# K and V blocks of 2 MB from one buffer arena, and wq and wo 2 MB at once, in a four-pass attention kernel

## The chip, the cores and the metric

The kernel runs on one core of one Trainium2 chip. The metric is the device time of the whole program in microseconds; lower is better. Engines are named as the profile names them: PE is TensorE (matmul), PEld its weight loads, DVE is VectorE, ACT is ScalarE, POOL is GpSimd, SP is SyncE, which issues the loads here. The build gives each engine a queue of instructions of its own; "DMA" means the 16 DMA engines of the core.

## The reference

Forward and backward of attention, MLP, attention, MLP for one token, with the same weights and the same K and V caches in both layers. What matters is the traffic: K and V are 4 heads x 65536 rows x 128 columns in bfloat16, 64 MiB each, and have to be read several times, because a softmax over all rows lies between them.

```python
x = x + A(layernorm(x), k_cache, v_cache, wq, wo)   # 32 query heads on 4 K/V heads, 65536 keys
x = x + B(layernorm(x), w1, b1, w2, b2)             # relu squared, 1024 -> 3584 -> 1024
x = x + A(layernorm(x), k_cache, v_cache, wq, wo)
x = x + B(layernorm(x), w1, b1, w2, b2)
# outputs: x and the gradients of all inputs (those of K and V are 64 MiB each)
```

The kernel goes over K and V four times: pass 1 and pass 2 are the forward attentions, pass 3 the backward of the second layer, pass 4 the rest with the stores of both cache gradients. Between the passes lie three dense phases with the MLP weights.

## The kernel before

K, V, weights and outgoing blocks share 12 buffer parts of 1 MiB (8 KB in each of 128 partitions). A load is traced where its block is first used; SP runs ahead of the compute engines as far as parts and semaphores allow.

```python
    BLK = J * DH                                   # J = 32 rows of 128: 8 KB in a partition
    SLOTS = [(slotp, "slot%d" % i) for i in range(NSLOT)]     # NSLOT = 12
    ...
    def kv8(t, g, c8):                             # 8 chunks of a K or V block, loaded at its first use
        b, j = divmod(c8, J)
        key = (t, g, b)
        if key not in KV["have"]:
            sl = Slot("blk_" + t)
            v = sl.t[:, :].rearrange("p (j d) -> p j d", d=DH)
            nc.sync.dma_start(out=v, in_=KVIN[t][g][b])
            KV["have"][key] = (sl, v)
        return KV["have"][key][1][:, j:j + 8, :]
```

A forward pass is a software pipeline over groups of 8 chunks. `kT` transposes K on PE and copies the result out of PSUM on ACT or DVE (`evac` balances a load count); `kS` makes the scores from a copy two steps old. After every 16 groups `stats` finds the maximum and ACT computes 8 exponentials of 128x128. `v8` multiplies V by them 23 steps after the K of the same rows.

```python
        def kT(g, c8):
            kb8 = kv8("k", g, c8)
            pt = ps_tr()
            for i in range(8):
                nc.tensor.transpose(pt[:, i, :], kb8[:, i, :], ident_b[:, :])
            kv_done("k", g, c8)                    # gives the part back after its last use
            kt = ktpool.tile([P, 8, P], BF, name="kt", tag="kt")      # 4 buffers
            evac(kt[:, :, :], pt[:, :, :])         # ACT or DVE
            state[(g, c8)] = kt
        ...
        def stats(g, su):
            ...                                    # DVE, PE, DVE, PE, DVE: the maximum over partitions
            for h in range(R):                     # R = 8
                nc.scalar.activation(out=E(g, c0, SU)[:, :, L["lr"].start + h], in_=S[:, h, :], func=ACTF.Exp,
                                     bias=negm[:, g, su, h:h + 1], scale=SCALE, accum_out=rs[:, h:h + 1])
        ...
        pipeline(items, [(kT, 0), (kS, TLEAD), (v8, FWD_LAG)], bg, end)     # lags 0, 2, 23
```

Of the kernel before, what the change touches and what calls it, by code (L numbers as in the profile page):

```python
# [10 lines left out]
BF = mybir.dt.bfloat16  # L11
# [5 lines left out]
P = 128  # L17
# [3 lines left out]
def kernel(  # L21
# [24 lines left out]
    nc = tc.nc  # L46
    D = A_x.shape[-1]
    G = A_k_cache.shape[1]
    SK = A_k_cache.shape[2]
    DH = A_k_cache.shape[3]  # L50
    QD = A_wq.shape[1]
    HQ = QD // DH
    R = HQ // G
    F = B_w1.shape[1]
    DC, FC = D // P, F // P
    C = SK // P
    J = 32
    NB = C // J
    SU = min(128, C)
# [7 lines left out]
    STORE_STEPS = 5  # L67
    WAIT_STEPS = 5
    NSLOT = 12
# [6 lines left out]
    epool = ctx.enter_context(tc.tile_pool(name="epool", bufs=1))  # L76
    ktpool = ctx.enter_context(tc.tile_pool(name="ktpool", bufs=4))
    mvs = ctx.enter_context(tc.tile_pool(name="mvs", bufs=2))
    slotp = ctx.enter_context(tc.tile_pool(name="slotp", bufs=1))
# [14 lines left out]
    def ps_gg():  # L94
        return PS["pool"].tile([P, 512], F32, name="ps_gg", tag="gg", bufs=4)

    def ps_acc(shape):
        return PS["pool"].tile(shape, F32, name="ps_acc", tag="acc", bufs=1)
# [30 lines left out]
    load = {"act": 0.0, "dve": 0.0, "pe": 0.0}  # L129
# [108 lines left out]


    BLK = J * DH  # L240
    SLOTS = [(slotp, "slot%d" % i) for i in range(NSLOT)]
    FREE = [(0, i) for i in range(NSLOT)]
    NOW = {"step": 0}

    class Slot:
        def __init__(self, name, fill=False):
            n = 0
            if fill:
                ready = [k for k, (at, _) in enumerate(FREE) if at <= NOW["step"] - 1]
                n = ready[-1] if ready else 0  # L250
            self.i = FREE.pop(n)[1]
            pool, tag = SLOTS[self.i]
            self.t = pool.tile([P, BLK], BF, name=name, tag=tag)

        def free(self, stored=False):

            give_slot(self.i, STORE_STEPS if stored else 0)

    def give_slot(i, more=0):
        NOW["step"] += 0.01  # L260
        insort(FREE, (NOW["step"] + more, i))

    def add_slot(pool, tag):
        SLOTS.append((pool, tag))
        give_slot(len(SLOTS) - 1)

    def kv_views(ap):
        return [ap[0, g].rearrange("(b p j) d -> b p j d", p=P, j=J) for g in range(G)]

    KVIN = {"k": kv_views(A_k_cache), "v": kv_views(A_v_cache)}  # L270
    GKv = kv_views(out_2)
    GVv = kv_views(out_3)

    KV = {"have": {}, "keep": set()}

    def kv8(t, g, c8):
        b, j = divmod(c8, J)
        key = (t, g, b)
        if key not in KV["have"]:
            sl = Slot("blk_" + t)  # L280
            v = sl.t[:, :].rearrange("p (j d) -> p j d", d=DH)
            nc.sync.dma_start(out=v, in_=KVIN[t][g][b])
            KV["have"][key] = (sl, v)
        return KV["have"][key][1][:, j:j + 8, :]

    def kv_done(t, g, c8):

        key = (t, g, c8 // J)
        if c8 % J == J - 8 and key not in KV["keep"]:
            KV["have"].pop(key)[0].free()  # L290

    def order_by_unit(desc, unit):
        out = []
# [7 lines left out]
    def touch_order(items, stages):  # L301
        seen, out = set(), []
        maxlag = max(l for _, l in stages)
        for i in range(len(items) + maxlag):
            for t, lag in stages:
# [13 lines left out]
    TOUCH = [touch_order(ITEMS[0], [("k", 0), ("v", FWD_LAG)]), touch_order(ITEMS[1], [("k", 0), ("v", FWD_LAG)]),  # L319
             touch_order(ITEMS[2], [("v", 0), ("k", B3_LAG)]), touch_order(ITEMS[3], [("v", 0), ("k", B4_LAG)])]  # L320

    def plan_keep(p):
        if p == 3:
            return set()
        last = TOUCH[p][-(NKEEP + 2):]
        return set([k for k in TOUCH[p + 1] if k in last][:NKEEP])
# [9 lines left out]
    def rows_of(W):  # L336
        return W.rearrange("(kc p) n -> p kc n", p=P)
# [1 line left out]
    def f_rows_of(W):  # L339
        return W.rearrange("(s p j) n -> p s j n", p=P, j=4)  # L340

    def slabs(name, load, nk, kper, ncols, ahead=1):
        pend = deque()
        ks = deque(range(0, nk, kper))

        def fetch():
            k = ks.popleft()
            kn = min(kper, nk - k)
            sl = Slot(name)
            v = sl.t[:, 0:kn * ncols].rearrange("p (k n) -> p k n", n=ncols)  # L350
            nc.sync.dma_start(out=v, in_=load(k, kn))
            pend.append((k, kn, sl, v))

        def gen():
            while ks or pend:
                while ks and len(pend) < ahead:
                    fetch()
                k, kn, sl, v = pend.popleft()
                for kk in range(kn):
                    yield k + kk, v[:, kk, :]  # L360
                sl.free()
        g = gen()
        g_fetch = [fetch for _ in range(ahead)]
        return g, g_fetch
# [7 lines left out]

    def wq_slabs(g, ahead=1):
        v = rows_of(A_wq)
        return slabs("s_wq", lambda k, kn: v[:, k:k + kn, g * 1024:(g + 1) * 1024], DC, 4, 1024, ahead)

    def wo_slabs(g, ahead=1):
        v = rows_of(A_wo)
        return slabs("s_wo", lambda k, kn: v[:, g * R + k:g * R + k + kn, :], R, 4, 1024, ahead)

    def w1_slabs(ahead=1):
        v = rows_of(B_w1)
# [276 lines left out]
    def pipeline(items, stages, bg, end=()):  # L659
        maxlag = max(l for _, l in stages)  # L660
        for i in range(len(items) + maxlag):
            for fn, lag in stages:
                if 0 <= i - lag < len(items):
                    fn(*items[i - lag])
            bg.step(i)
            NOW["step"] += 1
            for before, fn in end:
                if i == len(items) + maxlag - before:
                    fn()
# [16 lines left out]
    EH = max(SU, C // 2)  # L686
    ETILE = {}
# [8 lines left out]
    def E_done(g, c0, n):  # L696

        if c0 % EH == 0 and EH * R2 == BLK:
            add_slot(epool, "E%d_%d" % (g, c0 // EH))

    def gsl(g):
        return slice(g * R, (g + 1) * R)
# [50 lines left out]
    def attn_fwd(p, L, on_group, bg, end=()):  # L753
# [3 lines left out]
        state = {}  # L757
# [121 lines left out]
                    nc.scalar.activation(out=L["fw"][:, g, :, :], in_=fd[:], func=ACTF.Exp)  # L879

        KV["keep"] = plan_keep(p)
        pipeline(items, [(kT, 0), (kS, TLEAD), (v8, FWD_LAG)], bg, end)
        st.close()

# [17 lines left out]
    def attn_bwd3(p, L, on_group, bg, end=()):  # L902
# [5 lines left out]
        state = {}  # L908
# [56 lines left out]
                    on_group(g)  # L965

        KV["keep"] = plan_keep(p)
        pipeline(items, [(vT, 0), (vS, TLEAD), (k8, B3_LAG)], bg, end)
        st.close()


    def attn_bwd4(p, La, Lb, on_group, bg, stack, end=()):
# [8 lines left out]
        state = {}  # L981
# [84 lines left out]
        def outer16(name, out, key, xt, gg, j1):  # L1066

            if j1 == 0:
                state[key] = Slot(name, True)
            stg = state[key].t[:, :].rearrange("p (j d) -> p j d", d=DH)  # L1070
            for m in range(2):
                pgs = [ps_gg(), ps_gg()]
                for h in range(2):
                    nc.tensor.matmul(pgs[h][:, :], lhsT=xt[64 * h:64 * h + 64, j1 // 8 + m, :],  # L1074
                                     rhs=gg[64 * h:64 * h + 64, :, :].rearrange("p a b -> p (a b)"),
                                     start=True, stop=True, tile_position=(64 * h, 0))
                for h in range(2):
                    jj = j1 + 8 * m + 4 * h
                    evac(stg[:, jj:jj + 4, :].rearrange("p j d -> p (j d)"), pgs[h][:, :], kind="f32")
            if j1 + 16 == J:  # L1080
                nc.gpsimd.dma_start(out=out, in_=stg)
                state.pop(key).free(stored=True)

        def dV8(g, c8):
            b, j0 = divmod(c8, J)
            if 2 * j0 < J:
                outer16("gstv", GVv[g][b], "stv", state[("xe", g, b)], state[("GG", g, c8 // SU)][1], 2 * j0)

        def k8(g, c8):
            kb8 = kv8("k", g, c8)  # L1090
            b, j0 = divmod(c8, J)
            su = c8 // SU
            X, xt = state[("xd", g, b)]
            if c8 == sufirst[(g, su)]:
                state["ps_dq"] = ps_acc([P, 4, R2])
            ps_dq = state["ps_dq"]
            for i in range(8):
                c = c8 + i
                s = c % J
                w = min(4, J - s)  # L1100
                nc.tensor.matmul(ps_dq[:, 0:w, :].rearrange("p a b -> p (a b)"), lhsT=kb8[:, i, :],  # L1101
                                 rhs=X[:, s:s + w, :].rearrange("p a b -> p (a b)"),
                                 start=(c == sufirst[(g, su)]), stop=(c == sulast[(g, su)] + 7), skip_group_check=True)
            kv_done("k", g, c8)
            if c8 == sulast[(g, su)]:
                fold_dq(La, g, su, ps_dq[:, 0, 0:R], gfirst[g] // SU == su, glast[g] // SU == su, dspool)
                if glast[g] // SU == su:
                    on_group(g)
            if 2 * j0 >= J:
                outer16("gstk", GKv[g][b], "stk", xt, state[("GG", g, su)][0], 2 * j0 - J)  # L1110

        KV["keep"] = plan_keep(p)
        pipeline(items, [(vT, 0), (vS, TLEAD), (dV8, DV_LAG), (k8, B4_LAG)], bg, end)


# [325 lines left out]
```

## Time and profile before

| | before |
|---|---|
| time, median of 3 runs | 2035.71 us (2035.61 to 2037.0) |
| moved by DMA | 803.5 MB, 395 GB/s over the span |
| DMA share in the passes | 1.01 (passes 1 to 3), 0.97 (pass 4) |
| PE busy | 83% of the span |

From the page of the kernel before: the engines' busy time, and the span in 40 slices (PEclk is the clock granted to TensorE, DMA the share in tenths, GB/s the rate).

```profile
span 2035.9 us, 69009 instructions
...
PE 1689.3 (83%) x30754; PEld 1344.3 (66%) x30754; DVE 1188.6 (58%) x2586; ACT 1103.0 (54%) x2063; POOL 92.4 (5%) x232
...
DMA  9999999999999998999999986999999999999995
GB/s 384 416 410 414 413 414 415 360 335 406 411 414 413 413 415 323 398 415 410 416 412 414 416 338 231 375 424 393 422 424 424 423 423 404 423 415 423 423 371 212
```

The rate is nearly flat within a pass, 410 to 416 GB/s in passes 1 to 3 and mostly 422 to 424 in pass 4, and falls most in the dense phases (the 360 335, 323 and 338 231) and at the end. The windows view gives passes 1, 2 and 3, from the first transpose to the last matmul on a cache block; the last three columns are PE's clock, DMA share and GB/s.

```profile
core 0: us, PE busy (x) PEld busy (x) DVE busy (x) ACT busy (x) POOL busy (x), PEclk, DMA share, GB/s
12.50:378.10 365.60, 296.47 (x6658) 280.70 (x6659) 168.10 (x387) 175.40 (x387) 0.29 (x1) 0.93 1.01 411
433.30:781.20 347.90, 285.60 (x6587) 270.76 (x6585) 165.89 (x382) 173.71 (x385) 0.29 (x1) 0.93 1.01 406
833.30:1197.70 364.40, 296.62 (x6510) 265.76 (x6506) 170.96 (x327) 151.06 (x186) 0.67 (x1) 0.96 1.01 412
```

PE has 60 to 70 us of idle time in each forward pass. The waits view of PE says for what it waited (us in total, times, longest), and SP's own waits say what held the next load back.

```profile
PE ps_sc L792 <- DVE kt L153: 38.8, 26, 2.4
...
PE ps_sc L792 <- ACT kt L150: 11.5, 33, 1.8
...
PE ps_tr L774 <- DMA blk_k<-in_A_k_cache_dram: 3.3, 3, 1.4
```

```profile
SPq L282 <- DMA blk_k<-in_A_k_cache_dram: 215.3, 112, 4.3
SPq L282 <- DMA blk_v<-in_A_v_cache_dram: 206.8, 113, 4.4
...
SPq L282 <- PE ps_tr L774: 117.8, 77, 5.4
```

Of the waits before a load of K or V, those for earlier loads to land are the longest (422 us together; the waits of SP for stores, such as 279.9 us for `gstv`, belong to pass 4), and the DMA share is 1.01: DMA is the limit. In pass 2 alone (433.3 to 781.2 us) SP already waits longer for PE to give parts back, 146 us, than for loads, 84 us:

```profile
SPq L282 <- PE ps_acc L858: 76.2, 31, 8.1
SPq L282 <- PE ps_tr L774: 70.1, 41, 5.1
SPq L282 <- DMA blk_k<-in_A_k_cache_dram: 43.1, 22, 2.1
SPq L282 <- DMA blk_v<-in_A_v_cache_dram: 40.6, 23, 3.1
```

PE hardly ever waits for a K block (3.3 us in two passes).

### The profile page before, as it was taken

How to read it: one execution, taken by the hardware profiler on the slowest of the kernel's cores; microseconds unless marked ns; L12 is line 12 of the kernel's file. 1: busy time of each engine (PE TensorE's matmuls, PEld its weight loads, DVE VectorE, ACT ScalarE, POOL GpSimd, SP SyncE). 2: the span in 40 equal slices, each digit the busy share in tenths (PEclk: the TensorE clock that was granted, in tenths of full speed). 3: DMA queues.
4: the chain of work that ended last, by engine and by line, in shares of the span. 5: the costliest groups of instructions: out<-in, count | busy, mean ns of one | idle time of the engine just before them, and what ended most of it. 6: DMA issues, size and time to landing. Idle time of an engine off the chain costs nothing.

```text
span 2035.9 us, 69009 instructions
## 1 busy us (share of the span) xinstructions
PE 1689.3 (83%) x30754; PEld 1344.3 (66%) x30754; DVE 1188.6 (58%) x2586; ACT 1103.0 (54%) x2063; POOL 92.4 (5%) x232
## 2 busy tenths in 40 slices
PE   7888887688788886887978888979988978898897
PEld 6778777688787776776867777545544545454454
DVE  4444454255444542555464446867967877687775
ACT  3544454255444542445354345767766766576675
POOL 0000000000000000000000000101101111010111
PEclk9999899799899996999999988988988998698898
DMA  9999999999999998999999986999999999999995
GB/s 384 416 410 414 413 414 415 360 335 406 411 414 413 413 415 323 398 415 410 416 412 414 416 338 231 375 424 393 422 424 424 423 423 404 423 415 423 423 371 212
DMA packets 136536, 803.50 MB, mean 395 GB/s; under 512 B 12448, under 2 KB 12462, under 8 KB 52398
## 3 DMA queue, kind: packets, MB, share of 16 engines
q1 hardware_dynamic: 112190, 633.39, 76.9%
q0 software_dynamic: 24048, 165.70, 19.6%
q8 instruction: 240, 3.93, 0.8%
q14 instruction: 58, 0.48, 0.1%
HBM read 633.35 MB, written 165.69 MB: 392 GB/s over the span
## 4 chain that ended last, share of the span: by engine, by line
PE 45%; DMA 28%; ACT 15%; DVE 8%; issue 4%; SPq 0%; ACTq 0%; POOLq 0%; DVEq 0%; POOL 0%
DMA blk_v<-in_A_v_cache_dram 13%; PE ps_tr L774 7%; ACT E L831 6%; DMA blk_k<-in_A_k_cache_dram 5%; PE ps_sc L792 5%; PE ps_tr L1026 4%; PE ps_gg L1074 4%; PE ps_acc L858 4%; ACT kt L150 4%; PE ps_tr L917 3%; DVE kt L153 3%; DMA out_dram<-og 3%; PE ps_gg L1139 2%; DMA out_dram<-gstk 2%; PE ps_mv L397 2%
## 5 line engine op out<-in xcount | busy, mean ns | idle before, releaser
L153 DVE COPY kt<-ps_tr 128x1024 bf16<-128x1024 bf16 x751 | 507.3, 687 | 340.6 <-PE ps_tr L774 145.4
L150 ACT COPY kt<-ps_tr 128x1024 bf16<-128x1024 bf16 x273 | 275.7, 1024 | 410.9 <-PE ps_tr L774 230.0
L774 PE MATMUL ps_tr<-ident_b,blk_k 128*128 128x128 bf16 x4096 | 297.3, 226 | 4.3 <-DMA blk_k<-in_A_k_cache_dram 3.3
L150 ACT CAST gstk<-ps_gg 128x512 bf16<-128x512 f32 x396 | 207.6, 600 | 99.7 <-PE ps_gg L1074 78.5
L150 ACT CAST gstv<-ps_gg 128x512 bf16<-128x512 f32 x379 | 199.2, 601 | 100.1 <-PE ps_gg L1074 99.2
L774 PEld LDWEIGHTS <-blk_k 128*128 128x128 bf16 x4096 | 249.5, 102 | 4.9 <-DMA blk_k<-in_A_k_cache_dram 3.8
L792 PE MATMUL ps_sc<-L_qpad,kt 128*128 128x64 bf16 (+7 forms) x4096 | 197.4, 194 | 52.8 <-DVE kt L153 38.8
L1074 PE MATMUL ps_gg<-GG,xt 64*128 64x512 bf16 x1024 | 211.5, 403 | 21.2 <-ACT gstk L150 11.0
L792 PEld LDWEIGHTS <-kt 128*128 128x128 bf16 x4096 | 158.8, 100 | 71.3 <-DVE kt L153 45.7
L858 PE MATMUL ps_acc<-E,blk_v 128*128 128x64 bf16 (+4 forms) x4096 | 177.6, 200 | 33.0 <-issue 10.9
L1026 PEld LDWEIGHTS <-blk_v 128*128 128x128 bf16 x2048 | 128.5, 103 | 108.0 <-issue 83.0
L1026 PE MATMUL ps_tr<-ident_b,blk_v 128*128 128x128 bf16 x2048 | 183.0, 230 | 20.1 <-DMA blk_v<-in_A_v_cache_dram 18.9
L858 PEld LDWEIGHTS <-blk_v 128*128 128x128 bf16 x4096 | 152.9, 103 | 36.4 <-issue 31.3
L831 ACT ACTIVATE E<-S_sb,L_negm 128x128 bf16<-128x128 f32 x256 | 150.4, 990 | 38.2 <-DVE L_negm L827 38.1
L1101 PEld LDWEIGHTS <-blk_k 128*128 128x128 bf16 x2048 | 84.3, 100 | 115.7 <-issue 87.0
L917 PE MATMUL ps_tr<-ident_b,blk_v 128*128 128x128 bf16 x2048 | 143.7, 224 | 14.3 <-DMA blk_v<-in_A_v_cache_dram 12.0
L917 PEld LDWEIGHTS <-blk_v 128*128 128x128 bf16 x2048 | 121.4, 100 | 31.1 <-DMA blk_v<-in_A_v_cache_dram 20.6
L1101 PE MATMUL ps_acc<-X,blk_k 128*128 128x64 bf16 (+3 forms) x2048 | 119.2, 196 | 23.0 <-DMA blk_k<-in_A_k_cache_dram 23.0
L831 ACT ACTIVATION_READ_ACCUMULATOR E<-S_sb,L_negm 128x1 f32 x256 | 123.5, 483 | 0.0
L937 PE MATMUL ps_sc<-dOpad,kt 128*128 128x64 bf16 (+7 forms) x2048 | 100.7, 194 | 26.6 <-ACT kt L150 15.5
L1055 PE MATMUL ps_sc<-DOB,kt 128*128 128x64 bf16 (+3 forms) x2048 | 111.3, 198 | 0.2 <-DVE kt L153 0.2
L153 DVE CAST gstv<-ps_gg 128x512 bf16<-128x512 f32 x133 | 90.0, 684 | 28.1 <-PE ps_gg L1074 27.7
(271 smaller groups left out, 2203.0 us busy)
## 6 DMA issues: line engine op xcount, KB each, us to landing
blk_k<-in_A_k_cache_dram SPq DMA_DIRECT2D x248, 1024.0 KB, 20.1
blk_v<-in_A_v_cache_dram SPq DMA_DIRECT2D x243, 1024.0 KB, 20.2
out_dram<-gstv POOLq DMA_DIRECT2D x64, 1024.0 KB, 13.1
out_dram<-gstk POOLq DMA_DIRECT2D x64, 1024.0 KB, 12.5
s_wq<-in_A_wq_dram SPq DMA_DIRECT2D x32, 1024.0 KB, 18.8
s_wo<-in_A_wo_dram SPq DMA_DIRECT2D x32, 1024.0 KB, 20.2
s_w<-in_B_w_dram SPq DMA_DIRECT2D x32, 896.0 KB, 7.8
out_dram<-og POOLq DMA_DIRECT2D x23, 1024.0 KB, 13.9
```

The source lines that it names most:

```text
L150: nc.scalar.copy(out=out, in_=in_)
L153: nc.vector.tensor_copy(out=out, in_=in_)
L774: nc.tensor.transpose(pt[:, i, :], kb8[:, i, :], ident_b[:, :])
L792: nc.tensor.matmul(state["ps_s"][:, s:s + w, :].rearrange("p a b -> p (a b)"), lhsT=kt[:, i, :], rhs=L["qpad"][:, g, 0:w, :].rearrange("p ...
L831: nc.scalar.activation(out=E(g, c0, SU)[:, :, L["lr"].start + h], in_=S[:, h, :], func=ACTF.Exp, bias=negm[:, g, su, h:h + 1], scale=SCALE ...
L858: nc.tensor.matmul(ps_o[:, 0:w, :], lhsT=vb8[:, i, :], rhs=E(g, c, w)[:, :, lr], start=(c % SU == 0), stop=(c % SU == SU - 1), skip_group_ ...
L917: nc.tensor.transpose(pt[:, i, :], vb8[:, i, :], ident_b[:, :])
L937: nc.tensor.matmul(state["ps_dp"][:, s:s + w, :].rearrange("p a b -> p (a b)"), lhsT=vt[:, i, :], rhs=dOpad[:, g, 0:w, :].rearrange("p a b ...
L1026: nc.tensor.transpose(pt[:, i, :], vb8[:, i, :], ident_b[:, :])
L1055: nc.tensor.matmul(state["ps_dp"][:, s:s + w, :].rearrange("p a b -> p (a b)"), lhsT=vt[:, i, :], rhs=DOB[:, g, 0:w, :].rearrange("p a b - ...
L1074: nc.tensor.matmul(pgs[h][:, :], lhsT=xt[64 * h:64 * h + 64, j1 // 8 + m, :], rhs=gg[64 * h:64 * h + 64, :, :].rearrange("p a b -> p (a b) ...
L1101: nc.tensor.matmul(ps_dq[:, 0:w, :].rearrange("p a b -> p (a b)"), lhsT=kb8[:, i, :], rhs=X[:, s:s + w, :].rearrange("p a b -> p (a b)"), ...
```

## The change

The intent is fewer, larger DMA packets. A K or V block may now take two neighbouring parts of an arena, with one load of 16 KB per partition. If no pair is free, if the block's other half is there already, or in pass 4, halves are loaded as before. In the passes wq and wo also come 2 MB at once (their packets stay 2 KB). For this the rows of a block are laid out so that a half is an 8 KB run at a 16 KB pitch in DRAM. Dense weights take the part that has been free longest.

```diff
-    SLOTS = [(slotp, "slot%d" % i) for i in range(NSLOT)]
-    FREE = [(0, i) for i in range(NSLOT)]
+    JW = 2 * J
+    ARENA = slotp.tile([P, NSLOT * BLK], BF, name="arena")
+    GRAN = [ARENA[:, i * BLK:(i + 1) * BLK] for i in range(NSLOT)]
+    FREE = {i: 0.0 for i in range(NSLOT)}
+    def take_pair():
+        both = [(max(FREE[i], FREE[i + 1]), i) for i in range(0, NSLOT, 2) if i in FREE and i + 1 in FREE]
+        ...
     def kv_views(ap):
-        return [ap[0, g].rearrange("(b p j) d -> b p j d", p=P, j=J) for g in range(G)]
+        return [ap[0, g].rearrange("(b p j) d -> b p j d", p=P, j=JW) for g in range(G)]
     ...
+            if NOW["pairs"] and hb % 2 == 0 and (t, g, hb + 1) not in have:
+                i = take_pair()
+            if i is None:
+                sl = Slot("blk_" + t)
+                nc.sync.dma_start(out=sl.t.rearrange("p (j d) -> p j d", d=DH), in_=half(KVIN[t], g, hb))
+                have[key] = sl
+            else:
+                for h in range(2):
+                    have[(t, g, hb + h)] = Slot("blk_" + t, at=i + h)
+                if key in KV["halves"]:            # the last blocks of a pass: two 1 MB loads
+                    ...
+                else:
+                    nc.sync.dma_start(out=wide(i).rearrange("p (j d) -> p j d", d=DH), in_=KVIN[t][g][hb // 2])
     ...
 # slabs() for wq and wo: 2 * kper rows in a pair, where NOW["wide"]
     ...
     def pipeline(items, stages, bg, end=()):
         for i in range(len(items) + maxlag):
+            NOW["wide"] = NOW["pairs"]
     ...
+        NOW["pairs"] = p < 3
```

The hunks left out adapt names, the gradients' views and the freeing of pairs.

More of the change, by code (lines that the diff above doesn't have):

```diff
@@ L240 @@
     BLK = J * DH
-    SLOTS = [(slotp, "slot%d" % i) for i in range(NSLOT)]
-    FREE = [(0, i) for i in range(NSLOT)]
-    NOW = {"step": 0}
-    class Slot:
-        def __init__(self, name, fill=False):
-            n = 0
-            if fill:
-                ready = [k for k, (at, _) in enumerate(FREE) if at <= NOW["step"] - 1]
-                n = ready[-1] if ready else 0
-            self.i = FREE.pop(n)[1]
-            pool, tag = SLOTS[self.i]
-            self.t = pool.tile([P, BLK], BF, name=name, tag=tag)
+    JW = 2 * J
@@ new lines, with wide @@
+    ARENA = slotp.tile([P, NSLOT * BLK], BF, name="arena")
+    GRAN = [ARENA[:, i * BLK:(i + 1) * BLK] for i in range(NSLOT)]
+    FREE = {i: 0.0 for i in range(NSLOT)}
+    NOW = {"step": 0, "pairs": True, "wide": False}
+    def wide(i):
+        return ARENA[:, i * BLK:(i + 2) * BLK]
+    def take_pair():
+        both = [(max(FREE[i], FREE[i + 1]), i) for i in range(0, NSLOT, 2) if i in FREE and i + 1 in FREE]
+        if not both:
+            return None
+        i = min(both)[1]
+        del FREE[i], FREE[i + 1]
+        return i
@@ new lines, in take_one, with __init__ @@
+    def take_one(fill):
+        by_age = sorted((t, i) for i, t in FREE.items())
+        if fill:
+            ready = [i for t, i in by_age if t <= NOW["step"] - 1]
+            i = ready[-1] if ready else by_age[0][1]
+        else:
+            i = by_age[0][1]
+        del FREE[i]
+        return i
+    class Slot:
+        def __init__(self, name, fill=False, at=None, both=False):
+            self.i = take_one(fill) if at is None else at
+            self.n = 2 if both else 1
+            self.t = wide(self.i) if both else GRAN[self.i]
@@ L255, in free, with add_slot @@
         def free(self, stored=False):
-            give_slot(self.i, STORE_STEPS if stored else 0)
+            for k in range(self.n):
+                give_slot(self.i + k, STORE_STEPS if stored else 0)
     def give_slot(i, more=0):
         NOW["step"] += 0.01
-        insort(FREE, (NOW["step"] + more, i))
-    def add_slot(pool, tag):
-        SLOTS.append((pool, tag))
-        give_slot(len(SLOTS) - 1)
+        FREE[i] = NOW["step"] + more
+    def add_slot(view):
+        GRAN.append(view)
+        give_slot(len(GRAN) - 1)
@@ L267, in kv_views, with half @@
     def kv_views(ap):
-        return [ap[0, g].rearrange("(b p j) d -> b p j d", p=P, j=J) for g in range(G)]
+        return [ap[0, g].rearrange("(b p j) d -> b p j d", p=P, j=JW) for g in range(G)]
     KVIN = {"k": kv_views(A_k_cache), "v": kv_views(A_v_cache)}
+    def half(views, g, hb):
+        return views[g][hb // 2][:, J * (hb % 2):J * (hb % 2) + J, :]
     GKv = kv_views(out_2)
     GVv = kv_views(out_3)
-    KV = {"have": {}, "keep": set()}
+    KV = {"have": {}, "keep": set(), "halves": set()}
@@ L276, in kv8 @@
     def kv8(t, g, c8):
-        b, j = divmod(c8, J)
-        key = (t, g, b)
-        if key not in KV["have"]:
-            sl = Slot("blk_" + t)
-            v = sl.t[:, :].rearrange("p (j d) -> p j d", d=DH)
-            nc.sync.dma_start(out=v, in_=KVIN[t][g][b])
-            KV["have"][key] = (sl, v)
-        return KV["have"][key][1][:, j:j + 8, :]
+        hb, j = divmod(c8, J)
+        key = (t, g, hb)
+        have = KV["have"]
+        if key not in have:
+            i = None
+            if NOW["pairs"] and hb % 2 == 0 and (t, g, hb + 1) not in have:
[8 more added lines that the diff above has]
+                if key in KV["halves"]:
+                    for h in range(2):
+                        nc.sync.dma_start(out=GRAN[i + h].rearrange("p (j d) -> p j d", d=DH), in_=half(KVIN[t], g, hb + h))
+                else:
+                    nc.sync.dma_start(out=wide(i).rearrange("p (j d) -> p j d", d=DH), in_=KVIN[t][g][hb // 2])
@@ L286, in kv_done @@
+        return have[key].t.rearrange("p (j d) -> p j d", d=DH)[:, j:j + 8, :]
     def kv_done(t, g, c8):
@@ L289, in kv_done @@
         if c8 % J == J - 8 and key not in KV["keep"]:
-            KV["have"].pop(key)[0].free()
+            KV["have"].pop(key).free()
     def order_by_unit(desc, unit):
@@ L340, in f_rows_of, with slabs @@
         return W.rearrange("(s p j) n -> p s j n", p=P, j=4)
-    def slabs(name, load, nk, kper, ncols, ahead=1):
+    def slabs(name, load, nk, kper, ncols, ahead=1, flat=False):
         pend = deque()
@@ L347, in fetch @@
             k = ks.popleft()
-            kn = min(kper, nk - k)
-            sl = Slot(name)
+            i = None
+            if ks and flat and NOW["wide"]:
+                i = take_pair()
+            if i is None:
+                kn = min(kper, nk - k)
+                sl = Slot(name)
+            else:
+                kn = min(2 * kper, nk - k)
+                ks.popleft()
+                sl = Slot(name, at=i, both=True)
             v = sl.t[:, 0:kn * ncols].rearrange("p (k n) -> p k n", n=ncols)
@@ L374, in wq_slabs @@
         v = rows_of(A_wq)
-        return slabs("s_wq", lambda k, kn: v[:, k:k + kn, g * 1024:(g + 1) * 1024], DC, 4, 1024, ahead)
+        return slabs("s_wq", lambda k, kn: v[:, k:k + kn, g * 1024:(g + 1) * 1024], DC, 4, 1024, ahead, True)
     def wo_slabs(g, ahead=1):
         v = rows_of(A_wo)
-        return slabs("s_wo", lambda k, kn: v[:, g * R + k:g * R + k + kn, :], R, 4, 1024, ahead)
+        return slabs("s_wo", lambda k, kn: v[:, g * R + k:g * R + k + kn, :], R, 4, 1024, ahead, True)
     def w1_slabs(ahead=1):
@@ L665, in pipeline @@
             bg.step(i)
+            NOW["wide"] = False
             NOW["step"] += 1
@@ L698, in E_done @@
         if c0 % EH == 0 and EH * R2 == BLK:
-            add_slot(epool, "E%d_%d" % (g, c0 // EH))
+            add_slot(ETILE[(g, c0 // EH)][:, :])
     def gsl(g):
@@ L881, in attn_fwd @@
         KV["keep"] = plan_keep(p)
+        NOW["pairs"] = p < 3
+        KV["halves"] = set(TOUCH[p][-4:])
         pipeline(items, [(kT, 0), (kS, TLEAD), (v8, FWD_LAG)], bg, end)
@@ L967, in attn_bwd3 @@
         KV["keep"] = plan_keep(p)
+        NOW["pairs"] = p < 3
+        KV["halves"] = set(TOUCH[p][-4:])
         pipeline(items, [(vT, 0), (vS, TLEAD), (k8, B3_LAG)], bg, end)
@@ L1086, in dV8 @@
             if 2 * j0 < J:
-                outer16("gstv", GVv[g][b], "stv", state[("xe", g, b)], state[("GG", g, c8 // SU)][1], 2 * j0)
+                outer16("gstv", half(GVv, g, b), "stv", state[("xe", g, b)], state[("GG", g, c8 // SU)][1], 2 * j0)
         def k8(g, c8):
@@ L1109, in k8 @@
             if 2 * j0 >= J:
-                outer16("gstk", GKv[g][b], "stk", xt, state[("GG", g, su)][0], 2 * j0 - J)
+                outer16("gstk", half(GKv, g, b), "stk", xt, state[("GG", g, su)][0], 2 * j0 - J)
         KV["keep"] = plan_keep(p)
+        NOW["pairs"] = p < 3
+        KV["halves"] = set(TOUCH[p][-4:])
         pipeline(items, [(vT, 0), (vS, TLEAD), (dV8, DV_LAG), (k8, B4_LAG)], bg, end)
```

## The prediction

> **What bounds it now.** The DMA engines. In the windows view the passes move 413 to 416 GB/s (100 to 350 us, 500 to 750, 850 to 1150) at a DMA share of 1.02, and 420 GB/s in the last pass (1500 to 1900); PE is busy 83% of 500 to 700 and waits little on loads. About 100 of the 2035.9 us lie in dips: the dense phases (342 to 359 GB/s at 350 to 450, 351 and 368 at 750 to 850, 305 and 238 at 1200 to 1300) and the tail (177 in the last 36 us).
>
> **What the change does to that rate.** In the trace's packet records (passes 1 to 3) an 8192-byte packet takes 313 ns (median), a 2048-byte packet 84 to 87, and each load ends with a 4-byte packet of 9 ns per engine. In the last pass 2048, 4096, 7168 and 8192 bytes take 84, 159, 272, 309 ns: about 9 ns plus 0.0367 ns per byte. The Trainium skill ("DMA: Bandwidth & Descriptors", "Why small descriptors are slow") tells of a fixed per-packet overhead; the trace agrees, with about 9 ns. A 16 KB packet should take some 617 ns in passes 1 to 3 instead of 2 x 313. Per engine a 2 MB load saves 8 x 8.5 ns and one 9 ns packet: 77 ns of 5.03 us, 1.5%; from 413 to about 419 GB/s.
>
> The DMA view shows 491 K and V loads, 370 of them in passes 1 to 3. The last blocks of each pass, the 7 kept blocks and moments without a free pair stay halves; I reckon with 165 pairs: 165 x 0.077 = 13 us, all on the bounding resource. The 2 MB wq and wo loads keep 2 KB packets: nothing. The last pass makes no pairs; its transfers become 8 KB runs at a 16 KB pitch in DRAM, which I expect to cost nothing (2 KB runs at a pitch show no penalty now).
>
> **What it may cost.** Now loads are limited to 8 in flight: the queue's own waits show SP waiting for earlier K and V loads (422 us), and a load lands after 20.1 us, 8 x 2.5. Afterwards the arena limits: 12 parts minus a K pair, a V pair and at times a weight pair leave 3 to 4 pairs ahead, 6 to 8 MB or 15 to 20 us, far above PE's waits (5 us at most). So DMA should stay full inside the passes. A pair lands all at once: 2.5 us at each pass's start, partly hidden. Dense weights find the arena in another order: a few us either way. Together I take 1 us off.
>
> **Prediction: 2023 us, 8 in 10 between 2008 and 2037. Faster by over 2%: 0.04; within 2%: 0.92; slower by over 2%: 0.04.**
>
> **What would show it.** Some 21,000 packets of 16384 bytes at 610 to 625 ns; some 165 K and V loads of 2048 KB in the DMA view; windows inside passes 1 to 3 at 418 to 421 GB/s; last pass and dips as before within 5 us.
>
> **What would make it wrong.** 16 KB packets no cheaper per byte: about 2036. Few pairs found because kept blocks and weights split the arena. In-flight depth falling so far that DMA has gaps in the passes (share under 1.0). The new pitch slowing the last pass. Waits falling on whole pairs, so that the dips grow.

## More of the kernel before

A scheduler of the build may move an instruction ahead of others on its engine if its inputs are expected sooner. The built order can be listed engine by engine.

## The result, and the profile after

| | before | after |
|---|---|---|
| median of 3 runs | 2035.71 us | 2093.45 us (2087.09 to 2096.24) |
| ratio | | 1.0271, 95% interval 1.0245 to 1.0297 |
| profiled run | 2035.9 us | 2085.3 us |

The kernel became 2.7% slower. First what the change was made for: the load groups of the DMA view of the changed kernel (KB each, median us from issue to landing).

```profile
arena<-in_A_k_cache_dram SPq DMA_DIRECT2D x93, 2048.0 KB, 15.1
arena<-in_A_v_cache_dram SPq DMA_DIRECT2D x86, 2048.0 KB, 16.2
```

There are 179 pairs, and the trace's packet records say what a packet took (all loads of the kernel):

```
bytes    before: packets, median ns    after: packets, median ns
    4         9759       9                  6607       9
 2048        32768      84                 32768      84
 8192        65536     313                 19712     309
16384            0       -                 22912     614
```

A 16 KB packet takes 614 ns and replaces two of 313 ns. (The 309 ns after are no gain of the layout: most 8 KB packets left are those of pass 4, which took 309 ns before as well.) Where pairs run undisturbed the gain is there: 425 GB/s in place of 416 in the stretch from 50 to 100 us. Now the page and the three passes of the changed kernel.

```profile
span 2085.3 us, 68814 instructions
...
DMA  9999999578999997899999998699999999999995
GB/s 390 424 415 395 394 402 404 216 299 357 414 423 379 420 406 286 311 394 420 421 416 424 419 401 303 257 421 424 415 423 423 422 423 392 424 424 423 417 384 208
```

```profile
19.00:400.80 381.80, 298.23 (x6598) 284.31 (x6595) 169.64 (x384) 174.90 (x386) 0.29 (x1) 0.89 0.95 388
461.30:834.40 373.10, 296.60 (x6584) 284.92 (x6585) 168.38 (x380) 174.12 (x385) 0.29 (x1) 0.88 0.93 380
887.10:1249.40 362.30, 297.53 (x6510) 274.73 (x6506) 172.43 (x327) 151.56 (x186) 0.67 (x1) 0.91 1.00 414
```

Passes 1 and 2 are 16 and 25 us longer and DMA is idle in them (share 0.95 and 0.93); PE does the same work in them with more idle time and at a lower granted clock (0.89 and 0.88 against 0.93). Pass 3 is 2 us shorter, and pass 4 is unchanged (757.4 before, 756.2 after). Measured by the ends of the passes, which leaves no gap between the stretches, the time to the end of pass 1 went from 378.1 to 400.8 us and from there to the end of pass 2 from 403.1 to 433.6: these two stretches hold +53 us, all of the loss.

```profile
PE ps_sc L838 <- ACT kt L150: 72.9, 51, 4.4
...
PE ps_sc L838 <- DVE kt L153: 4.7, 5, 1.7
```

```profile
SPq L319 <- PE ps_tr L820: 361.9, 53, 12.5
...
SPq L319 <- PE ps_acc L904: 186.8, 47, 9.8
```

SP no longer waits for loads but for PE to give parts back. And PE does not wait for loads; it waits for copies of `kt` by ACT, 72.9 us in place of 11.5, up to 4.4 us at once. Its waits for DVE's copies fell meanwhile from 38.8 to 4.7 us, so the net is 27 us more. In the three windows above PE is also busy 13 us longer in passes 1 and 2, at the lower clock; the two sizes together are about the 41 us by which these passes grew. One such wait in pass 2, in order of time (start, us, what; engines as they come):

```profile
631.81 1.51 PE L820 MATMUL ps_tr<-ident_b,arena 128*128 128x128 bf16 x24
...
632.17 0.85 ACT L877 ACTIVATE E<-S_sb,L_negm 128x128 bf16<-128x128 f32 x1 [2.81 <-DVE L_negm L873]
...
635.80 0.98 ACT L877 ACTIVATE E<-S_sb,L_negm 128x128 bf16<-128x128 f32 x1
...
636.44 1.20 ACT L150 COPY kt<-ps_tr 128x1024 bf16<-128x1024 bf16 x1
636.84 0.17 DVE L888 TENSOR_TENSOR zn<-z,al 128x8 f32<-128x8 f32 x1 [4.46 <-ACT al L886]
...
637.12 1.28 DVE L153 COPY kt<-ps_tr 128x1024 bf16<-128x1024 bf16 x2
...
637.70 0.61 PE L838 MATMUL ps_sc<-L_qpad,kt 128*128 128x64 bf16 x8 [4.38 <-ACT kt L150]
638.12 1.04 PE L820 MATMUL ps_tr<-ident_b,arena 128*128 128x128 bf16 x8
...
642.76 0.61 PE L820 MATMUL ps_tr<-ident_b,arena 128*128 128x128 bf16 x8
```

The transposes, three groups of 8, are done at 633.3. ACT has to copy one group and DVE the other two. ACT's copy stands behind all 8 exponentials and starts at 636.4; PE stands still for 4.4 us. DVE's two copies are late too, at 637.1: they stand behind a small DVE instruction that waits for `al`, a small exponential that ACT also runs after the 8. The Trainium skill, "PSUM — Partial Sum Buffer", section "Engine vs sequencer instructions", calls the queues of ScalarE and VectorE "strict FIFO"; this trace agrees, the copy waits 3.1 us with its input ready.

Afterwards PE's clock is at half: 8 transposes take 1.04 us in place of 0.61 until about 642. The skill's "TensorE: Matmul & The Clock Gate", section "HAM oscillation — how this bites in real kernels", gives the rule of no PE gaps over about 3.4 us. Here the gap was 4.38 us and the clock records have the half clock from 635.4 to 642.2, so it began 2.1 us after PE had stopped. All 15 PE gaps over 3.4 us of the changed kernel between 19.0 and 834.4 us have half clock within them or up to 1.1 us after them, and so far the trace agrees with the rule. But shorter gaps do not keep the clock: of the 24 stretches of half clock in the kernel before (12.5 to 781.2 us, 116 us in all) 22 had no gap over 2.9 us in the 6.8 us ahead of them, and of the 33 in the changed kernel (191 us in all) 20 had none over 3.2 us.

### The profile page after: what moved, and what is told of

The parts are those of the page before. It is cut to its first block, busy times and chain, and to the rows that moved or that the text cites. A ratio compares the mean times of both kernels' runs of the same rounds, so it can differ in the third digit from the quotient of the medians.

```text
span 2085.3 us, 68814 instructions
## 1 busy us (share of the span) xinstructions
PE 1709.9 (82%) x30754; PEld 1374.1 (66%) x30754; DVE 1195.8 (57%) x2586; ACT 1103.3 (53%) x2063; POOL 92.4 (4%) x232
## 4 chain that ended last, share of the span: by engine, by line
PE 48%; DMA 24%; ACT 15%; DVE 8%; issue 4%; ACTq 0%; POOLq 0%; DVEq 0%; POOL 0%; SPq 0%
PE ps_tr L820 9%; DMA arena<-in_A_v_cache_dram 8%; ACT E L877 6%; DMA out_dram<-arena 6%; PE ps_sc L838 6%; PE ps_acc L904 4%; PE ps_tr L1076 4%; PE ps_gg L1124 4%; PE ps_tr L965 3%; ACT kt L150 3%; DMA arena<-in_A_k_cache_dram 3%; ACT arena L150 2%; PE ps_gg L1191 2%; DMA E<-in_A_v_cache_dram 2%; PE ps_sc L985 2%
## 5 line engine op out<-in xcount | busy, mean ns | idle before, releaser
L150 ACT CAST arena<-ps_gg 128x512 bf16<-128x512 f32 x715 | 375.2, 600 | 161.6 <-PE ps_gg L1124 140.9
L820 PE MATMUL ps_tr<-ident_b,arena 128*128 128x128 bf16 x4096 | 331.9, 234 | 11.0 <-DMA arena<-in_A_k_cache_dram 5.6
L838 PE MATMUL ps_sc<-L_qpad,kt 128*128 128x64 bf16 (+7 forms) x4096 | 216.6, 197 | 80.0 <-ACT kt L150 72.9
L820 PEld LDWEIGHTS <-arena 128*128 128x128 bf16 x4096 | 268.0, 106 | 13.3 <-issue 7.1
L153 DVE CAST arena<-ps_gg 128x512 bf16<-128x512 f32 x294 | 198.7, 685 | 67.7 <-PE ps_gg L1124 36.6
L838 PEld LDWEIGHTS <-kt 128*128 128x128 bf16 x4096 | 174.8, 102 | 94.5 <-ACT kt L150 82.9
L904 PE MATMUL ps_acc<-E,arena 128*128 128x64 bf16 (+4 forms) x4096 | 163.8, 199 | 33.7 <-issue 14.0
L965 PE MATMUL ps_tr<-ident_b,arena 128*128 128x128 bf16 x2048 | 162.4, 232 | 18.9 <-DMA arena<-in_A_v_cache_dram 18.5
L904 PEld LDWEIGHTS <-arena 128*128 128x128 bf16 x4096 | 148.2, 103 | 35.2 <-issue 34.7
L1076 PEld LDWEIGHTS <-arena 128*128 128x128 bf16 x1728 | 108.4, 103 | 87.9 <-issue 69.4
L1076 PE MATMUL ps_tr<-ident_b,arena 128*128 128x128 bf16 x1728 | 154.3, 231 | 14.4 <-DMA arena<-in_A_v_cache_dram 13.3
L965 PEld LDWEIGHTS <-arena 128*128 128x128 bf16 x2048 | 130.8, 105 | 33.0 <-DMA arena<-in_A_v_cache_dram 24.8
L150 ACT CAST E<-ps_gg 128x512 bf16<-128x512 f32 (+1 forms) x197 | 104.4, 606 | 49.1 <-PE ps_gg L1124 40.9
L985 PE MATMUL ps_sc<-dOpad,kt 128*128 128x64 bf16 (+7 forms) x2048 | 108.1, 196 | 21.4 <-DVE kt L153 11.7
L1151 PEld LDWEIGHTS <-arena 128*128 128x128 bf16 x1600 | 65.9, 100 | 83.4 <-issue 67.8
L985 PEld LDWEIGHTS <-kt 128*128 128x128 bf16 x2048 | 85.7, 101 | 30.2 <-DVE kt L153 12.7
```

Source lines behind the costliest of these rows:

```text
L150: nc.scalar.copy(out=out, in_=in_)
L153: nc.vector.tensor_copy(out=out, in_=in_)
L838: nc.tensor.matmul(state["ps_s"][:, s:s + w, :].rearrange("p a b -> p (a b)"), lhsT=kt[:, i, :], rhs=L["qpad"][:, g, 0:w, :].rearrange("p ...
L904: nc.tensor.matmul(ps_o[:, 0:w, :], lhsT=vb8[:, i, :], rhs=E(g, c, w)[:, :, lr], start=(c % SU == 0), stop=(c % SU == SU - 1), skip_group_ ...
L965: nc.tensor.transpose(pt[:, i, :], vb8[:, i, :], ident_b[:, :])
L985: nc.tensor.matmul(state["ps_dp"][:, s:s + w, :].rearrange("p a b -> p (a b)"), lhsT=vt[:, i, :], rhs=dOpad[:, g, 0:w, :].rearrange("p a b ...
```

## The experiments

The first suspects were the order in which the build queued the instructions, and the depth of the loads. In both kernels the traced order of PE's 30,694 matmuls is the same, but only 46% of the positions in passes 1 and 2 of the built order agree: the changed kernel has the matmuls of `v8` in longer runs (59 runs of 40 or more, 4 before). The rivals: ORDER (the new order slows PE), DEPTH (pairs occupy the arena so that too few loads are in flight), LAYOUT (the pitch in DRAM, or the arena as one tile, costs).

An order is imposed with edges for the build alone, which make an instruction queue behind another and add no wait:

```python
for a, b in zip(order, order[1:]):     # positions in the traced order; passes 1 and 2
    tc.add_manual_dep(pe[b], pe[a].name, DependencyInfo(DependencyClass.NoSync, DependencyReason.DATA), reason="pin")
```

### Old order on the new loads, new order on the old loads, no pairs, pairs as halves

```diff
 # e1: the changed kernel         # e2: the kernel before
+order = PE order of before       +order = PE order of the changed kernel
 # e3
-        NOW["pairs"] = p < 3      # three places, and the initial value
+        NOW["pairs"] = False
 # e4
-                if key in KV["halves"]:
+                if True:                           # every pair: two loads of 1 MB
```

> The changed kernel, its loads and buffers untouched, but TensorE's instructions of passes 1 and 2 queued in exactly the order of the kernel before (issue order only). ORDER theory (the build's scheduler reacted to the 2 MB loads by bunching the V matmuls into long runs, and that order makes the TensorE-ScalarE chain slower than the DMA): passes 1 and 2 lose most of their 41 us, total 2025 to 2045 us, DMA share in the passes back to 1.0. DEPTH theory (pairs hold the buffer longer, too few loads are in flight to cover TensorE's stalls): stays at 2075 to 2095 us.

> The kernel before, 1 MB loads, with TensorE's instructions of passes 1 and 2 queued in the changed kernel's order. ORDER theory: 2065 to 2095 us, with the long waits of TensorE for ScalarE's kt copies. DEPTH theory: 2033 to 2042 us, as before.

> The changed kernel with no pairs taken at all: arena, 8 KB runs at a 16 KB pitch in DRAM, 1 MB loads; the order of the V matmuls comes out as before (240 runs, mean 17). ORDER and DEPTH both say 2030 to 2042 us. A LAYOUT theory (the pitch in DRAM, or the arena as one tile, costs) says over 2060 us.

> The changed kernel, pairs of buffer parts taken as there, but each pair filled by two 1 MB loads. The scheduler's order is between the two (228 runs of V matmuls, 36 of them of 40 or more, against 4 before and 59 in the changed kernel). ORDER theory: 2050 to 2080 us. DEPTH theory in its form that pairs hold the buffer: 2075 to 2095 us; in its form that a 2 MB load lands too late: 2033 to 2045 us.

| run | median us | ratio to before (95%) |
|---|---|---|
| e1, new loads, old PE order | 2042.36 | 1.0039 (1.0018 to 1.0060) |
| e2, old loads, new PE order | 2032.18 | 0.9991 (0.9969 to 1.0014) |
| e3, arena, no pairs | 2035.14 | 1.0013 (0.9988 to 1.0039) |
| e4, pairs as two 1 MB loads | 2083.59 | 1.0240 (1.0215 to 1.0265) |

LAYOUT fell with e3. The late landing of a 2 MB load is not the cause either: with 1 MB loads e4 is nearly as slow. (e4's time lies in the range of DEPTH and 3.6 us above that of ORDER; the count below explains it.) DEPTH alone fell with e1: the same loads and buffers under the old order lose almost nothing. But ORDER as stated fell with e2: PE's new order alone is free. A new theory was formed, INTERPLAY: bunched V matmuls need more loads ahead than pairs leave. It had a weak spot: pinning PE let the build reorder ACT and DVE, so that e2 had PE's order of the changed kernel but not that of ACT.

### All three engines in the new order; ACT and DVE as in e2; nine parts

```diff
 # e5: the kernel before; PE, ACT and DVE pinned to the changed kernel's order
 # e6: the changed kernel; PE, ACT and DVE pinned to e2's order
 # e7 and e8: the kernel before, PE pinned to before's (e7) or the changed kernel's order (e8)
-    NSLOT = 12
+    NSLOT = 9
-    NKEEP = 7
+    NKEEP = 4
```

> The kernel before, 1 MB loads, with the instructions of TensorE, ScalarE and VectorE of passes 1 and 2 all queued in the changed kernel's order (the second run pinned TensorE alone and cost nothing: 2032 us). If the order of the copies and exponentials on ScalarE is the cause, whatever the loads: 2065 to 2095 us. If the order costs only together with pairs (the INTERPLAY theory: bunched V matmuls need more loads ahead than pairs leave): 2028 to 2042 us.

> The changed kernel with TensorE in its own order (bunched V matmuls), but ScalarE and VectorE in the order of the second run, which was fast. SCALARE-ORDER theory: 2030 to 2050 us. INTERPLAY theory (bunched V matmuls times pairs): 2070 to 2095 us.

> The kernel before with 9 buffer parts of 1 MB in place of 12 and 4 kept blocks in place of 7 (9 MB more to load, some 22 us), TensorE pinned to the kernel before's order. INTERPLAY theory: the smooth order lives with few parts: 2050 to 2070 us. If depth alone matters, whatever the order: over 2080 us.

> The same 9 parts and 4 kept blocks with TensorE pinned to the changed kernel's order. INTERPLAY theory: 20 us or more slower than the run with the old order, all of it in passes 1 and 2. If depth alone or the order of ScalarE matters: within 8 us of that run.

| run | median us | ratio to before (95%) |
|---|---|---|
| e5, old loads, all engines in the new order | 2073.47 | 1.0190 (1.0169 to 1.0211) |
| e6, new loads, ACT and DVE as in e2 | 2041.01 | 1.0032 (1.0009 to 1.0055) |
| e7, 9 parts, old PE order | 2060.76 | 1.0125 (1.0102 to 1.0148) |
| e8, 9 parts, new PE order | 2061.45 | 1.0129 (1.0107 to 1.0152) |

INTERPLAY fell three times: the slow order is slow with 1 MB loads (e5), the changed loads are fast with PE's bunched order (e6), and with 9 parts the two PE orders cost the same (e7, e8; the 25 us are about what the 9 MB more should cost). With 1 MB loads depth was not short: even with 9 parts (e7) pass 1 took 365.7 us, as before (365.6).

What separates the fast runs from the slow ones is the place of one copy. The built order of ACT was read for each of the 32 groups of exponentials in passes 1 and 2: how many of the 8 stand ahead of a `kt` copy that the program traced earlier?

```
                       0 ahead   1 to 4   5 to 7   all 8   median us
before, e1                30        0        0        2    2035.71, 2042.36
e2, e6                    10       20        0        2    2032.18, 2041.01
changed kernel, e5        10        1        5       16    2093.45, 2073.47
```

The traces of the other runs give the same count when ACT's instructions are taken in order of time: e3 and e7 are as before, e8 is as e2, and e4, slow with 1 MB loads, has 10, 1, 0 and 21.

### That queue position alone

Two runs put constraints on ACT's queue alone; the build then orders the rest. e9 pins no whole order: it adds one kind of edge to the changed kernel. e11 gives the kernel before the changed kernel's ACT order; it takes PE's order from the build again, which keeps the old runs (4 of 40 or more; 91% of the matmuls of passes 1 and 2 keep their place in the trace).

```diff
 # e9
+            LAST["kt"] = <the last kt copy that evac put on ACT>
 ...
-                nc.scalar.activation(out=E(g, c0, SU)[...], in_=S[:, h, :], func=ACTF.Exp, ...)
+                ex = nc.scalar.activation(out=E(g, c0, SU)[...], in_=S[:, h, :], func=ACTF.Exp, ...)
+                if h >= 2 and LAST.get("kt") is not None:
+                    queue_behind(ex.ins, LAST["kt"])       # one such NoSync edge
```

> The changed kernel with one constraint on ScalarE's queue and nothing else: in each group of 8 exponentials of passes 1 and 2, the third to eighth are queued behind the kt copy that the program made before them (in the built order no kt copy then has more than 2 exponentials ahead of it; in the changed kernel 16 groups have all 8 ahead, 5 have 6). COPY-BEHIND theory (that one queue position costs the 50 us): 2032 to 2048 us. If more of ScalarE's or VectorE's order matters: over 2060 us.

> The kernel before with ScalarE alone queued in the changed kernel's order in passes 1 and 2 (TensorE's order stays its own, loads 1 MB). COPY-BEHIND theory: 2060 to 2085 us, with TensorE waits of up to 4.4 us for kt copies of ScalarE and a lower granted clock in passes 1 and 2. If it takes TensorE's bunched order as well: 2030 to 2045 us.

e9 took 2037.73 us, ratio 1.0010 (0.9995 to 1.0024); e11 took 2079.99 us, ratio 1.0215 (1.0196 to 1.0234). The waits of PE for ACT's copies in passes 1 and 2, first the two slow runs (e5, then e11), then the two fast ones (e6, then e9):

```profile
PE ps_sc L816 <- ACT kt L174: 73.8, 55, 4.4
```

```profile
PE ps_sc L800 <- ACT kt L158: 73.2, 60, 3.8
```

```profile
PE ps_sc L861 <- ACT kt L173: 24.8, 49, 1.2
```

```profile
PE ps_sc L845 <- ACT kt L155: 14.6, 28, 1.2
```

The long waits come and go with the queue position and not with the loads. In e9's timeline of ACT the copy stands behind the second exponential, as constrained:

```profile
583.53 0.97 ACT L884 ACTIVATE E<-S_sb,L_negm 128x128 bf16<-128x128 f32 x1
...
584.16 1.20 ACT L155 COPY kt<-ps_tr 128x1024 bf16<-128x1024 bf16 x1
585.27 0.85 ACT L884 ACTIVATE E<-S_sb,L_negm 128x128 bf16<-128x128 f32 x1
```

One caution about e9: its constraint is on the copy of K, but the build was free to move other things. In e9's trace it also moved `al` ahead of the third exponential, and with it DVE's copies that had waited for `al`. So e9 alone does not tell ACT's copy from `al`. e11, the reverse on the other kernel, does. In its passes 1 and 2 DVE waits 44 us for `al` (35 in the kernel before, 73 in the changed kernel), and DVE's copies can run while PE waits for ACT's copy alone, as here:

```profile
601.45 1.28 DVE L161 COPY kt<-ps_tr 128x1024 bf16<-128x1024 bf16 x2
...
602.19 0.34 PE L782 MATMUL ps_tr<-ident_b,blk_k 128*128 128x128 bf16 x3 [0.86 <-DVE kt L161]
...
604.39 1.30 ACT L158 COPY kt<-ps_tr 128x1024 bf16<-128x1024 bf16 x1
...
605.74 0.41 PE L800 MATMUL ps_sc<-L_qpad,kt 128*128 128x64 bf16 x8 [3.21 <-ACT kt L158]
```

And in e6, which is fast, `al` still stands behind all 8 exponentials (though DVE's copies are queued ahead of the instruction that waits for it). How much of the changed kernel's loss the late copies of DVE add was not measured.

### The rest: pairs at the start of a pass

With the copy ahead the changed kernel only equals the kernel before, so the 13 us of the packets are still missing. A part of them shows in pass 1, whose end in e9 comes at 374.7 us in place of 378.1. More than that is given back before the end of pass 2: 415.2 us in place of 403.1. Windows of 10 us at the start of pass 2, from 420 to 430, in the kernel before and in e9:

```profile
420.00:430.00 10.00, 8.39 (x145) 8.13 (x143) 2.27 (x14) 4.31 (x5) 0.55 (x11) 0.90 0.85 314
```

```profile
420.00:430.00 10.00, 8.40 (x132) 8.14 (x130) 2.26 (x14) 3.30 (x4) 0.55 (x11) 0.83 0.14 54
```

DMA share 0.14 against 0.85: the dense weights still hold single parts, and the first loads of the pass wait until both parts of a pair are free. The edit makes the first 32 steps of each pass take single parts:

```diff
 # e10, on top of e9
+            NOW["pairs"] = pairs and i >= 32
             NOW["wide"] = NOW["pairs"]
 # e12, on top of e10
-            NOW["wide"] = NOW["pairs"]
+            NOW["wide"] = False
```

> As the run before, and in each pass no pairs and no 2 MB weights in the first 32 steps. TRANSITION theory (after a dense phase the first loads of pass 2 wait until both parts of a pair are free: about 9 us at the start of pass 2, some 5 at that of pass 3): 2022 to 2032 us, faster than the kernel before. If the gaps at the transitions have another cause: 2036 to 2045 us.

> As the tenth run, and wq and wo in the passes 1 MB at once. They save one 9 ns packet in a pair and hold two parts twice as long: 0 to 4 us faster than the tenth run if holding matters, the same within 2 us if not.

e10 took 2028.68 us (2024.94 to 2032.97), ratio 0.9961 (0.9948 to 0.9975). It beats both kernels, the one before by about 8 us (the interval excludes 1, though the gain is under 2%). The window from 420 to 430 us moves 283 GB/s again:

```profile
420.00:430.00 10.00, 8.39 (x159) 8.13 (x157) 2.27 (x14) 3.37 (x5) 0.55 (x11) 1.00 0.82 283
```

The stretch to the end of pass 2 fell from 415.2 (e9) to 405.5 us, 9.7 us as expected; the one to the end of pass 3 fell by 1.9 us where 5 were expected. e12 took 2029.23 us, ratio 0.9961 (0.9947 to 0.9976): the 2 MB weights gain and lose nothing.

## Why the prediction was wrong

- **Packets: right.** 617 ns were predicted for 16 KB, 614 measured; 165 pairs predicted, 179 measured. The rate of pass 3's middle (900 to 1100 us) went from 414 to 419 GB/s.
- **Layout: right.** 8 KB runs at a 16 KB pitch cost nothing (e3: 1.0013), and pass 4 stayed at its time.
- **"So DMA should stay full inside the passes": wrong, and this is the step that failed.** The reasoning compared the loads ahead (15 to 20 us) with PE's longest wait of the kernel before (5 us) and took PE's work as given. The change itself made new waits on PE, where no byte count shows it: the build queued a `kt` copy behind up to 8 exponentials on ACT. No single one of these waits is over 4.4 us; what counts is that there are 51 of them, which loads ahead cannot make up for once PE takes longer for a pass than DMA. The DMA share fell to 0.95 and 0.93 in passes 1 and 2. The queue position costs 50 us or so: the ratio fell from 1.0271 to 1.0010 when that place was put right (e9), 0.0261 x 2036 = 53 us, and giving the kernel before the changed ACT order costs 2.15%, 44 us (e11).
- **PE "waits little on loads": true, but read the wrong way.** PE's 17% of idle time was taken for room. PE did not wait for loads in the kernel before because it was itself nearly as slow as the loads: in pass 2 SP waited longer for PE (146 us) than for loads (84 us). With longer waits and the half clock that followed, it became the limit, gave parts back late, and DMA ran dry behind it.
- **In-flight depth** was named as a risk. It was tested in three ways and is not the cause: e1, e6, and nine parts in e7 and e8.
- **"A few us either way" in the dips: too small.** Pairs at the start of a pass cost about 10 us (e9 to e10, 0.0049 x 2036), more than was set aside for the start of passes and the dips together (1 us). That waits might fall on whole pairs stood in the list of risks, without a size.
- **Net of these, 8 of the 13 us appear** (e10, with 167 pairs of 16 KB packets). Not all 8 need be the packets': no run gave the kernel before e9's ordering edges with its own loads. At least part of the rest is lost early in pass 2: in the stretch from pass 1's end to pass 2's end the DMA share is 0.97 in e10 against 0.99 before, which is some 8 us more of idle DMA (an estimate from rounded shares, 0.02 x 405), and from the first transpose of pass 2 to 480 us the share is 0.87 (from 430.5) against 0.99 (from 433.3). Why is not shown.

Left open: why the build's scheduler moves the copy. It does so when pairs are taken, also when each is filled by two 1 MB loads (e4), and not when none is (e3, where ACT's order is that of before to the last instruction). So it goes with the holding of the pairs and not with the size of the load, but how the scheduler weighs it was not observed.

## What to carry to other kernels

If a build schedules instructions, a change of buffers or loads can change the order on engines that it does not touch. After such a change compare each engine's built order, and look for short copies that others wait for standing behind a group of long instructions; one ordering edge may be worth more than the change. And an engine that hardly waits for loads but is idle a fifth of the time is not an engine with room: ask how much longer its own work and waits may become before it is slower than the loads.

## What the Trainium skill lacked or had wrong

- "DMA: Bandwidth & Descriptors", "Why small descriptors are slow": it speaks of a fixed overhead of about 3 cycles per packet. Here 2048, 8192 and 16384 bytes took 84, 309 and 614 ns in the changed kernel (medians), which is 4 to 9 ns a packet, depending on the two sizes compared. The passage gives no clock for these cycles, so the two cannot be compared; it gives the penalty for small descriptors, and no figure for what 8 KB packets still gain (1 to 2%: 414 to 419 GB/s in pass 3, 416 to 425 in pass 1).
- "TensorE: Matmul & The Clock Gate", "HAM oscillation — how this bites in real kernels": the rule of gaps over about 3.4 us is not enough to keep the clock. In the kernel before, 22 of 24 stretches of half clock in passes 1 and 2 (12.5 to 781.2 us) came without any PE gap over 2.9 us in the 6.8 us before them.
- "DMA: Bandwidth & Descriptors", "Latency and other measured facts": its row pitches start at 512 KiB. 8 KB runs at a 16 KB pitch cost nothing (ratio 1.0013, e3).
- The pages say that queues are FIFO, but none read says to compare the built order of the engines after a change of buffers; here that order was worth 2 to 2.6% (e9, e11).
